# Sparse attention and a gated MLP on one core: the scores of batches 1 to 3 in three parts instead of four, under another listed order

## The chip, the cores and the metric

The kernel runs on one core of a Trainium2 chip. The metric is the device time of one execution in microseconds (us). Three executions of the kernel before took 216.66, 216.99 and 217.43 us, so the median is 216.99 us.

The engines are named as the profile names them: PE is TensorE (matmuls and transposes), PEld its weight loads, ACT is ScalarE, DVE is VectorE, POOL is GpSimd and SP is SyncE. In this kernel POOL issues the loads from HBM, and SP issues the stores and a set of moves inside the chip. Each engine has its own instruction queue and executes it in order; between engines only semaphores order the work.

## The reference

```python
B, H, S, D = q.shape                      # 4, 8, 768, 64
block, window = (32, 16)
k_sum = k.reshape(B, H, nb, block, D).max(axis=3)       # nb = 24
v_sum = v.reshape(B, H, nb, block, D).mean(axis=3)
scores_l = scale * np.matmul(q, k.transpose(0, 1, 3, 2))
mask_l = np.abs(pos[:, None] - pos[None, :]) < window
scores_s = scale * np.einsum('bhsd,bhnd->bhsn', q, k_sum) + np.log(block)
a = softmax(concatenate([where(mask_l, scores_l, -1e9), scores_s]))
attn = np.matmul(a, concatenate([v, v_sum]))
x = attn.transpose(0, 2, 1, 3).reshape(B * S, H * D)    # 3072 x 512
h = x @ w_in                                            # 512 -> 2048
g = h * np.clip(h + 3.0, 0.0, 6.0) / 6.0
out = g @ w_out                                         # 2048 -> 512
```

(The softmax is abbreviated here.) Each query sees the 31 keys around it and 24 block maxima, so the scores are a band and a narrow dense part.

## The kernel before, in words

**Attention.** The 768 queries of a head are cut into `NQ = 12` blocks of `QB = 64`. For a block, `kaug[p]` holds 120 key columns: 96 keys around it (`WIN`) and the 24 block maxima. `p` counts the four pairs of heads. The scores of a block come out with the keys on the partitions; `exp` (ACT) writes them as bf16 into the probabilities `at[p]`, and a multiplication by a band mask (DVE, "masking") zeroes what lies outside the window. `values` multiplies them with `vaug` (values, block sums and a column of ones), divides by the sum on DVE ("recip", "scale") and brings the result into `x`, the transposed input of the MLP. `half` 0 covers blocks 6 to 11, `half` 1 blocks 0 to 5.

Batch 0 has functions of its own (`k_step`, `q_step`, `scores`, `values_first`, `vsum_first`). Batches 1 to 3 use `turn` (tags `w`: 32x32 transposes of keys and queries on DVE, and the maxima), `scores4` (tags `s`, two pairs at once), `vsum` (tags `u4` to `u6`) and `values` (tags `v`).

**MLP.** The 3072 rows are 8 stages `s` of 384 (two per batch). `f1` (tags `F{s}x{ft}`, 16 per stage) is four matmuls into a PSUM bank `h` (there are three), a ReLU on ACT into `r` and the gate on DVE into `g`. `f2` (tags `G{s}{ts}x0`, three per stage, each in four quarters of four matmuls) accumulates in the one bank `o`; a copy and a store by SP follow. For stages 4 to 7 `x` is not made by PE transposes but by a DVE block transpose ("blocks", L642) and 16 small DMAs ("move", L648): four tokens of four DMAs, all on SP's queue. `F4` waits for the moves of batch 2, half 0; `F5`, `F6` and `F7` for the next ones.

**PSUM.** Two double banks `S` serve scores, values, sums and transposes. `scores4` takes both at once.

**The order.** Nothing is scheduled by the compiler. `Plan` records every operation under a tag and a number (`s100.1` is the first `exp` of that score block), and `issue` writes them out in the sequence of the string `ORDER`, which fixes each engine's queue. A suffix `:A` or `:D` picks ACT or DVE where both can do it. Tokens that begin with `-`, `~`, `_` or `=` are matmuls on an idle tile (`keep`, L782), which compute nothing. Loads have tokens too: `K`, `Q` and `V` are keys, queries and values of a batch, `Q0w` the queries of batch 0 for its second half, `I` and `O` the two weight matrices. All of these are on POOL's queue, in the order listed.

Of the kernel before, what the change touches and what calls it, by code (L numbers as in the profile page):

```python
# [29 lines left out]
c.0 K00.0 c.7 c.17 c.6 c.8:A K01.0 c.10:D c.5 c.1 _40 -15 k0.0 k0.2:A c.18 ~1 =2 k1.0 K02.0 ~12 =3 k2.0 k3.0 c.15:D c.2 c.3  # L30
s000.0 k0.3:A c.13:D c.4 c.11:A k1.1 Q00.0 q0.0 k1.4 k0.1 c.20 k1.2:A Q01.0 ~2 =5 q1.0 k0.4 k1.3:D c.9:A c.14:A c.19 k2.3:A
q0.1:A s000.1 q0.2:A =1 s010.0 s010.1 k2.2:A k3.2:D k3.3:D k3.1 V00.0 h000.0:D h001.0:D k2.1 k2.4 s000.2 ~2 =5 v00.0 V01.0 u0.0
h010.0:D s020.0 c.16 s010.2 q1.2:A u0.3:D u0.1:D u0.4:D v01.0 v01.1 v01.2 v00.1 q1.1:A V02.0 h020.0:A h021.0:A h011.0:A v00.2
s020.1 v01.3 v00.3 V03.0 u1.0 u1.3:A h030.0:D s030.0 k3.4 ~2 s030.1 u1.4:D v01.4 h031.0:D Q0w0.0 Q0w1.0 v01.5:D Q0w2.0 =1 q3.0
q3.1:D q2.0 u1.1:A u1.2:D s020.2 v02.0 v02.1 v02.2 s021.0 v02.3 s030.2 v03.0 v03.1 q2.1:A v03.2 s011.0 v03.3 v00.4 v00.5:D v02.4
s021.1 s011.1 s021.2 v03.4 v03.5:D s011.2 v02.5:A s031.0 s031.1 s001.0 s031.2 I2.0 F0x3.0 F0x3.1 F0x3.2 F0x3.3 F0x3.4 F0x3.5
I4.0 F0x6.0 F0x6.1 F0x6.2 F0x4.0 F0x4.1 F0x4.2 F0x4.3 v411.0 v411.1 F0x5.0 F0x4.4 F0x4.5 v411.2 s001.1 I8.0 u0.2:A s001.2 F0x8.0
F0x8.1 F0x8.2 F0x5.1 I0.0 F0x5.2 F0x11.0 F0x1.0 F0x11.1 F0x11.2 F0x1.1 F0x1.2 F0x1.3 F0x1.4 F0x1.5 v410.0 v410.1 F0x7.0 F0x7.1
F0x7.2 v410.2 F0x10.0 F0x10.1 I12.0 F0x13.0 F0x13.1 F0x15.0 F0x15.1 F0x13.2 F0x10.2 v411.3 v411.4:D v410.3 v410.4:A F0x15.2
F0x14.0 F0x14.1 F0x14.2 F0x9.0 F0x9.1 F0x9.2 F0x0.0 F0x0.1 F0x2.0 F0x2.1 K13.0 K10.0 c.12:A F0x0.2 K12.0 K11.0 w10.0 Q1w1.0  # L40
F1x14.0 F1x14.1 F1x14.2 F1x4.0 F1x4.1 F1x4.2 F1x2.0 F1x2.1 F1x2.2 w10.1:D F0x2.2 F0x2.3 F0x2.4 F0x12.0 F0x12.1 F0x12.2 F1x8.0
F1x8.1 F1x8.2 F1x1.0 F1x1.1 F1x1.2 F0x0.3 F0x0.4 F0x0.5 F0x2.5 F1x9.0 F1x9.1 F1x9.2 F1x5.0 F1x5.1 F1x5.2 F1x15.0 F1x15.1 w11.0
w11.2 F1x15.2 w11.3:D Q1w4.0 Q1w2.0 Q1w0.0 w10.2 w10.3:D q6.0 q6.1:A q7.0 q7.1:A F1x7.0 F1x7.1 w11.1:A F1x7.2 F1x12.0 F1x12.1
F1x12.2 O0.0 G02x0.0 Q1w5.0 Q1w3.0 q4.0 q4.1:A q5.0 q5.1:A F1x6.0 F1x6.1 F1x6.2 O1.0 G02x0.1 s100.0 s100.1 s100.3 F1x3.0 w12.0
F1x11.0 F1x11.1 w13.0 w13.2 F1x3.1 F1x11.2 w12.2 w12.1:D O2.0 G02x0.2 s101.0 s101.1 O3.0 F1x10.0 G02x0.3 G02x0.4:A w13.3:D
w13.1:A s101.3 F1x0.0 G00x0.0 G00x0.1 w12.3:D s100.2 s101.2 s100.4 V10.0 h100.0:D F1x10.1 h110.0:A F1x10.2 F1x3.2 s110.0 s110.1
s110.2 s101.4 s110.3 G00x0.2 G00x0.3 G00x0.4:A V12.0 u4.0 h130.0:D h120.0:A F1x0.1 u4.1:D u4.2:A u4.4:D u4.3:D u4.5:D G02x0.5
G01x0.0 G01x0.1 G01x0.2 s110.4 F1x0.2 h111.0:A v100.0 v100.1 v100.2 h121.0:A v101.0 v101.1 v101.2 G01x0.3 G01x0.4:A K20.0 K21.0
K22.0 K30.0 K23.0 w21.0 F1x13.0 F1x13.1 F1x13.2 v100.3 v100.4:A w20.0 w21.3 G12x0.0 w21.2:A v101.3 v101.4:A V22.0 H2.0 h101.0:A
# [764 lines left out]
```

## Time and profile before

| | before |
|---|---|
| median of 3 executions | 216.99 us (216.66 to 217.43) |
| span of the profiled execution, first to last instruction | 215.4 us |
| PE busy | 207.6 us (96%) |
| DVE busy | 162.1 us (75%) |
| ACT busy | 136.0 us (63%) |
| POOL busy | 49.7 us (23%) |
| mean granted TensorE clock | 0.998 |
| read from HBM / written | 28.82 MB / 6.29 MB |

For the profiled execution the page gives the span alone; the span begins with its first instruction and ends with its last, and the median of the timed executions is 1.6 us above it. A busy share is an average over stages. A PE that is "busy" counts the latency of matmuls that overlap, so the pace of PE is better read from the chain of work that ended last: there a group of matmuls has the time by which it held up the next one.

### The profile page before, as it was taken

Reading aid. Unit: us, or ns where it says so; the run is one execution under the profiler, and the core shown is the slowest. Engines: PE = TensorE matmul, PEld = TensorE weight load, DVE = VectorE, ACT = ScalarE, POOL = GpSimd, SP = SyncE. Lnnn points to the kernel's source line nnn. Section 1 sums busy time; section 2 is a strip of 40 time slices with the busy share of each in tenths; the row PEclk is TensorE's granted clock in tenths of the full one; section 3 lists DMA queues with packets and bytes.
Section 4 is the critical chain, followed back from the end, with each engine's and each line's share of the span. In section 5 each row is a group of like instructions: output and inputs, shape, how many; then the busy total and the mean of one; then the engine's idle time right before and its main releaser. Section 6 shows DMA issues by size and latency. Waiting matters only on the chain.

```text
span 215.4 us, 6065 instructions
## 1 busy us (share of the span) xinstructions
PE 207.6 (96%) x2521; PEld 119.9 (56%) x2548; DVE 162.1 (75%) x318; ACT 136.0 (63%) x264; POOL 49.7 (23%) x66
## 2 busy tenths in 40 slices
PE   7999999999999999999999999999999999999993
PEld 7556656655555565565555555555555555564442
DVE  6889889999899999898899889887865555640021
ACT  3879778887898988756578696566345355520110
POOL 7968347905753244000000000000000000000000
PEclk9999999999999999999999999999999999999999
DMA  5999999999999999930334234113314300013123
GB/s 75 161 155 188 204 187 171 191 201 163 204 160 194 181 121 151 107 146 11 37 37 143 27 37 110 49 22 38 70 21 80 76 0 17 34 49 122 52 85 134
DMA packets 91724, 22.68 MB, mean 105 GB/s; under 512 B 82224, under 2 KB 88752, under 8 KB 91696
## 3 DMA queue, kind: packets, MB, share of 16 engines
q0 software_dynamic: 62288, 14.41, 71.9%
q1 hardware_dynamic: 29264, 7.80, 15.3%
q8 instruction: 20, 0.33, 0.6%
q10 hardware_dynamic: 144, 0.07, 0.1%
q14 instruction: 8, 0.07, 0.1%
HBM read 28.82 MB, written 6.29 MB: 163 GB/s over the span
## 4 chain that ended last, share of the span: by engine, by line
PE 82%; SPq 5%; DMA 4%; issue 2%; DVE 2%; POOL 2%; ACT 1%; ACTq 0%; POOLq 0%
PE h L666 36%; PE o L683 29%; PE h L683 5%; SPq L648 4%; DMA first<-in_q_dram 3%; PE S L623 3%; PE S L512 2%; DMA out_dram<-ot 1%; ACT vaug L241 1%; POOL first L305 1%; PE S L636 1%; PE S L666 1%; PE h L581 1%; PE S L489 1%; PE S L553 1%
## 5 line engine op out<-in xcount | busy, mean ns | idle before, releaser
L666 PE MATMUL h<-x,win 128*128 128x384 bf16 x500 | 91.1, 326 | 0.1
L670 ACT ACTIVATE r<-h 128x384 f32<-128x384 f32 x125 | 58.7, 492 | 38.8 <-PE h L666 36.8
L671 DVE SCALAR_TENSOR_TENSOR g<-r,h 128x384 bf16<-128x384 f32 x125 | 65.9, 546 | 22.6 <-ACT r L670 20.0
L683 PE MATMUL o<-wout,g 128*128 128x512 bf16 x309 | 78.0, 379 | 1.9 <-issue 0.8
L666 PEld LDWEIGHTS <-win 128*128 128x128 bf16 x512 | 48.7, 98 | 35.5
L683 PEld LDWEIGHTS <-g 128*128 128x128 bf16 x400 | 38.4, 98 | 37.6 <-issue 0.3
L520 ACT ACTIVATE at<-S 120x768 bf16<-120x768 f32 x24 | 18.6, 810 | 5.5 <-PE S L512 5.4
L241 ACT COPY ot<-o 128x512 f32<-128x512 f32 x17 | 10.0, 587 | 15.4 <-PE o L683 14.2
L521 DVE TENSOR_TENSOR at<-at,mask 96x768 bf16<-96x768 bf16 x24 | 12.6, 549 | 2.0 <-ACT at L520 1.6
L605 DVE TENSOR_TENSOR xn<-S,rc 128x768 bf16<-128x768 f32 x14 | 13.3, 950 | 0.3
L343 POOL DMA_DIRECT2D vaug<-in_v_dram x10 | 11.9, 1194 | 0.4 <-DMA first<-in_k_dram 0.2
L241 DVE COPY ot<-h 128x512 f32<-128x512 f32 x2 | 1.3, 686 | 13.7 <-PE h L683 13.7
L683 PE MATMUL h<-wout,g 128*128 128x256 bf16 (+1 forms) x64 | 11.4, 326 | 0.0
L467 DVE TENSOR_REDUCE red<-kaug 128x24 bf16<-128x768 bf16 x12 | 11.2, 943 | 0.1
L241 ACT COPY vaug<-vaug 32x640 bf16<-32x640 bf16 (+3 forms) x17 | 8.9, 574 | 0.6 <-DMA vaug<-in_v_dram 0.3
L241 ACT COPY vaug<-vs 24x1536 bf16<-24x1536 bf16 x6 | 8.8, 1468 | 0.6 <-DVE vs L241 0.5
L782 PE MATMUL o<-idle 128*128 128x64 bf16 (+2 forms) x70 | 7.5, 287 | 1.1 <-DVE idle L287 1.1
L455 DVE STREAM_TRANSPOSE kaug<-kraw 128x768 bf16<-128x768 bf16 x8 | 8.1, 1025 | 0.3 <-PE S L512 0.3
L623 PEld LDWEIGHTS <-at 120*64 120x64 bf16 x336 | 6.3, 111 | 3.0 <-issue 1.6
L333 POOL DMA_DIRECT2D kraw<-in_k_dram x8 | 5.9, 740 | 8.5 <-DVE kaug L455 7.4
L642 DVE STREAM_TRANSPOSE y<-xn 128x768 bf16<-128x768 bf16 x8 | 7.6, 965 | 0.2
L512 PEld LDWEIGHTS <-kaug 32*128 32x128 bf16 x576 | 5.3, 92 | 4.4 <-issue 3.6
(108 smaller groups left out, 184.2 us busy)
## 6 DMA issues: line engine op xcount, KB each, us to landing
out_dram<-ot SPq DMA_DIRECT2D x19, 256.0 KB, 2.3
vaug<-in_v_dram POOLq DMA_DIRECT2D x6, 384.0 KB, 12.9
wout<-in_moe_w_out_dram POOLq DMA_DIRECT2D x4, 512.0 KB, 9.9
win<-in_moe_w_in_dram POOLq DMA_DIRECT2D x3, 512.0 KB, 10.0
kraw<-in_k_dram POOLq DMA_DIRECT2D x8, 192.0 KB, 12.4
x<-y SPq DMA_DIRECT2D x64, 24.0 KB, 2.0
first<-in_k_dram POOLq DMA_DIRECT2D x6, 192.0 KB, 12.3
first<-in_q_dram POOLq DMA_DIRECT2D x6, 192.0 KB, 12.3
```

What stands on the lines that cost most here:

```text
L241: {"ACT": nc.scalar.copy, "DVE": nc.vector.tensor_copy, "POOL": nc.gpsimd.tensor_copy}[eng](o, i)
L343: op("POOL", "dma128", lambda: nc.gpsimd.dma_start(out=o[BLK:WIN, a:z, 0:D], in_=rows[:, a:z]), w=[("v", b % 2, c) for c in range(lo, hi)] ...
L467: op("DVE", "max", lambda: nc.vector.tensor_reduce(red.slot[:], w[:, :, BLK:WIN].rearrange("p t (n c) -> p t n c", n=2), axis=AX.X, op=ALU ...
L512: nc.tensor.matmul(X[g // 2].slot[:, g % 2, i * QB:(i + 1) * QB], kaug[2 * u + m][rows, t], qT[rows, 2 * u + m, t * QB:(t + 1) * QB], star ...
L520: op("ACT", "exp", lambda a=a, e=e: nc.scalar.activation(a, X[e].slot[0:KEYS, :, 0:HALF], AF.Exp, scale=scl), r=[X[e]], w=[("at", p, half)])
L521: op("DVE", "masking", lambda m=m: nc.vector.tensor_tensor(m, m, mask[:, low(half):low(half) + HQ].unsqueeze(1).to_broadcast([WIN, 2, HQ, ...
L605: nc.vector.tensor_tensor(o, src[..., 0:D], r.unsqueeze(len(r.shape)).to_broadcast(list(o.shape)), op=ALU.mult)
L623: nc.tensor.matmul(X.slot[64 * c:64 * c + 64, i, m:m + D + 1], a[:, t * QB:(t + 1) * QB], vaug[b % 2][0:KEYS, h, t, 0:D + 1], start=True, ...
L666: nc.tensor.matmul(bank(h)[:, 0:HALF], w_in_sb[:, kt, cols], xt[s].slot[:, kt], start=(kt == 0), stop=(kt == NP - 1))
L670: op("ACT", "relu", lambda: nc.scalar.activation(r.slot[:], bank(h)[:, 0:HALF], AF.Relu, bias=0.5, scale=1.0 / 6.0), r=[h], w=[r])
L671: op("DVE", "gate", lambda: nc.vector.scalar_tensor_tensor(gt[s].slot[:, ft], r.slot[:], 1.0, bank(h)[:, 0:HALF], op0=ALU.min, op1=ALU.mul ...
L683: nc.tensor.matmul(o.slot[:, a:z], gt[s].slot[:, ft, ts * 128:(ts + 1) * 128], w_out_sb[:, ft, a:z], start=(ft == 0), stop=(ft == NFT - 1))
```

## The change

`scores4` no longer goes by half and by two pairs. It goes by three parts. Part 0 takes pairs 0 and 1 over blocks 4 to 11, part 1 takes pairs 2 and 3 over the same blocks, and part 2 takes all four pairs over blocks 0 to 3. A part has 64 products of two matmuls in place of 48, fills the 512 columns of both halves of both `S` banks where 384 were filled, and is followed by two `exp` of 1,024 columns where there were two of 768. The masking is on 1,024 columns in parts 0 and 1 (two instructions), and on 512 in part 2 (four). The four tiles `at` become slices of one tile, so that one `exp` of part 2 can write two pairs. The dependencies are kept by three regions of `at`: `values` of half 0 waits for region 0 (parts 0 and 1), of half 1 for regions 1 and 2 (all parts). The copy "around" of the first 16 query columns, which only block 0 needs, now holds up part 2 alone.

Per batch this is 3 score steps in place of 4, 6 `exp` in place of 8, and 8 maskings as before. Over the kernel PE has the same products; there are 65 idle matmuls in place of 80. Where an operation may run on ACT or on DVE, some have changed sides. The whole string `ORDER` is another one. The pieces of it that matter here are shown, with what is left out between them.

```diff
+    THIRD = NQ // 3
-    at = [sb([128, 2, S], BF16, f"at{p}") for p in range(NP)]
+    ats = sb([128, NP, 2, S], BF16, "at")
+    at = [ats[:, p] for p in range(NP)]
...
-           r=[("q", p, 0)], w=[("q", p, 1)])
+           r=[("q", p, 0)], w=[("qa", p)])
+
+    def ats_of(p, half):
+        return [("at", p, x) for x in ((1, 2) if half else (0,))]
...
+    def scores4(b, part):
+        X = [Buf("S"), Buf("S")]
+        us, ts = ((0, 1), (0, THIRD)) if part == 2 else ((part,), (THIRD, NQ))
+        n = (ts[1] - ts[0]) * QB
+        cols = slice(ts[0] * QB, ts[1] * QB)
+        def mms():
+            for u in us:
+                for i, t in enumerate(range(*ts)):
+                    lo = us.index(u) * n + i * QB
+                    for m in range(2):
+                        for g in range(4):
+                            rows = slice(BLK * g, BLK * g + BLK)
+                            nc.tensor.matmul(X[g // 2].slot[:, g % 2, lo:lo + QB], kaug[2 * u + m][rows, t],
+                                             qT[rows, 2 * u + m, t * QB:(t + 1) * QB], start=m == 0, stop=m == 1)
...
+        for e in range(2):
+            ps_ = [2 * u + e for u in us]
+            o = ats[0:KEYS, ps_[0]:ps_[-1] + 1:2, :, cols]
+            op("ACT", "exp1024", lambda o=o, e=e: nc.scalar.activation(o, X[e].slot[0:KEYS].rearrange("p j (u c) -> p u j c", c=n), AF.Exp, scale=scl),
+               r=[X[e]], w=[("at", p, x) for p in ps_ for x in xs])
...
-        for half in range(2):
-            for u in range(2):
-                scores4(b, u, half)
+        for part in range(3):
+            scores4(b, part)
```

The order of the loads of batch 0 and of the first weights, before and after (other tokens left out):

```diff
-K00 K01 K02 Q00 Q01 V00 V01 V02 V03 Q0w0 Q0w1 Q0w2 I2 I4 I8 I0 I12 K13 K10 K12 K11 Q1w1 ...
+K01 K00 Q00 K02 Q01 V00 V01 Q0w1 Q0w0 Q0w2 V02 V03 I0 I4 I12 I8 K10 I2 K13 K11 K12 Q1w5 ...
```

Parts of the new `ORDER`: around the first `F0`, around `u4`, and ahead of `F4`, `F5` and `F6`.

```diff
+... q3.0 v00.1 v01.1 s020.2 q3.1:D s031.0 q2.0 v00.2 v00.3 v00.4 u1.0 I0.0 v01.2 v01.3 h011.0:A s030.2 s031.1 I4.0 s021.0 I12.0
+h020.0:D q2.1:D s001.0 I8.0 h030.0:D v03.0 v02.0 u1.1:A v02.1 v00.5:A u1.3:A v03.1 u1.2:D s001.1 s021.1 h031.0:A u1.4:D s031.2
+K10.0 v02.2 v03.2 v02.3 v03.3 F0x0.0 s011.0 v02.4 v03.4 v02.5:D I2.0 s021.2 K13.0 K11.0 K12.0 Q1w5.0 h021.0:A v01.4 Q1w0.0
+v01.5:D v03.5:D ~1 =1 v411.0 s001.2 F0x6.0 ...
+... s11.0 F1x5.1 s11.3 s11.1 V10.0 G00x0.0 Q20.0 G00x0.1 G00x0.2 G00x0.3 s10.4 h130.0:D s10.2 Q23.0 K22.0 F1x6.1 h120.0:D h121.0:A
+K21.0 F1x5.2 s11.4 h100.0:D s11.2 u4.0 G00x0.4:A h110.0:D u4.1:D u4.2:D u4.3:D G01x0.0 G01x0.1 u4.4:A v100.0 u4.5:D v101.0 ...
+... v201.0 v200.0 F3x10.0 F3x7.0 F3x2.0 G20x0.0 F3x7.1 F3x10.1 v201.1 v200.1 G20x0.1 w20.5:A v201.2 v200.2 v201.3 F3x7.2 F3x2.1
+w21.5:A F3x1.0 s22.0 F3x2.2 v200.3 F3x10.2 w30.1 F3x4.0 F3x1.1 s22.4 F3x4.1 v201.6 v201.7 F3x1.2 w31.0 F3x4.2 F3x9.0 G20x0.2 F3x9.1
+G20x0.3 G20x0.4:D G22x0.5 s22.1 F3x14.0 F3x14.1 s22.5 F3x11.0 s22.3 F3x14.2 s22.2 F3x11.1 w33.0 w31.3 w33.2:A G21x0.0 G21x0.1
+G21x0.2 G21x0.3 s22.6 F3x9.2 G21x0.4:A v201.5 F3x12.0 w31.1 F3x12.1 u6.0 v210.0 u6.1:A u6.4:A v211.0 w30.0 F3x11.2 F3x12.2 F3x8.0
+F3x8.1 F3x8.2 F3x15.0 F3x15.1 F3x15.2 w33.3 w32.0 w33.4:D v201.4 v211.1 G10x0.5 G20x0.5 G32x0.0 F3x13.0 F4x2.0 ...
+... v211.3 G32x0.4:A F4x15.0 F4x0.0 v210.2 ... v210.3 F4x14.0 ... v211.7 v211.4 ... v211.6 v211.5 ... F4x12.1 G31x0.4:A F5x10.0 ...
+... v301.2 G32x0.5 F5x4.0 F5x4.1 G42x0.2 v301.3 ... v301.5 G21x0.5 ... v301.4 ... G42x0.5 v301.7 v301.6 ... F5x12.0 F6x0.0 ...
```

More of the change, by code (lines that the diff above doesn't have):

```diff
@@ L29 @@
 ORDER = """
[L30 to L49, printed above, removed]
@@ new lines @@
+v02.0 u1.1:A v02.1 v00.5:A u1.3:A v03.1 u1.2:D s001.1 s021.1 h031.0:A u1.4:D s031.2 K10.0 v02.2 v03.2 v02.3 v03.3 F0x0.0 s011.0
+v02.4 v03.4 v02.5:D I2.0 s021.2 K13.0 K11.0 K12.0 Q1w5.0 h021.0:A v01.4 Q1w0.0 v01.5:D v03.5:D ~1 =1 v411.0 s001.2 F0x6.0
+u0.4:D s011.1 s011.2 h001.0:D F0x5.0 u0.2:A F0x6.1 F0x0.1 F0x0.2 F0x4.0 F0x0.3 v411.1 F0x5.1 F0x6.2 F0x0.4 Q1w2.0 c.14:A F0x4.1
+F0x4.2 F0x4.3 F0x15.0 F0x15.1 F0x4.4 F0x5.2 F0x0.5 v411.2 F0x12.0 F0x14.0 F0x15.2 F0x12.1 v410.0 Q1w4.0 Q1w3.0 F0x4.5 v410.1
@@ L494, in scores @@
         m = at[p][0:WIN, :, lo:lo + HALF].rearrange("p j (t c) -> p j t c", c=QB)
-        op("ACT", "exp", lambda: nc.scalar.activation(a, X.slot[0:KEYS, :, 0:HALF], AF.Exp, scale=scl), r=[X], w=[("at", p, half)])
+        op("ACT", "exp", lambda: nc.scalar.activation(a, X.slot[0:KEYS, :, 0:HALF], AF.Exp, scale=scl), r=[X], w=ats_of(p, half))
         if not masked:
```

125 lines of the change are left out of this document (66 added, 59 removed).

## The prediction

> **What bounds the kernel now.** I read the page first, then the busy times by stretch, the chain of work that ended last, the groups by form, and the queues of SP, DVE and POOL where the change moves something.
>
> ```profile
> span 215.4 us, 6065 instructions
> PE 207.6 (96%) x2521; PEld 119.9 (56%) x2548; DVE 162.1 (75%) x318; ACT 136.0 (63%) x264; POOL 49.7 (23%) x66
> DVE  6889889999899999898899889887865555640021
> PEclk9999999999999999999999999999999999999999
> ```
> ```profile
> 0.00:12.50 12.50, 10.97 (x157) 7.51 (x157) 9.58 (x32) 8.03 (x16) 10.79 (x21) 1.00 1.12 123
> 12.50:24.40 11.90, 11.30 (x294) 8.13 (x294) 9.86 (x30) 10.06 (x19) 8.06 (x11) 1.00 1.81 182
> 24.40:94.40 70.00, 68.66 (x976) 40.06 (x984) 64.98 (x118) 59.27 (x116) 30.81 (x35) 1.00 1.76 172
> 94.40:117.80 23.40, 23.08 (x337) 12.87 (x342) 21.30 (x40) 14.99 (x27) 0.00 (x0) 1.00 0.29 61
> 117.80:212.20 94.40, 93.60 (x773) 51.30 (x782) 56.07 (x101) 43.37 (x90) 0.00 (x0) 1.00 0.24 54
> ```
> ```profile
> 24.46 2.06 PE h L666 x12
> ...
> 57.77 0.84 PE S L553 x48
> ...
> 68.48 0.48 PE S L512 x48
> ...
> 74.04 0.65 PE h L666 x4
> 74.69 0.86 PE o L683 x4
> ...
> 94.37 0.88 PE S L623 x48
> ...
> 117.83 1.95 PE h L666 x12
> ...
> 210.83 1.32 PE h L683 x12
> ```
>
> The columns of the stretches are: length, busy time of PE, PEld, DVE, ACT and POOL with counts, granted clock, DMA share, GB/s. From 24.4 us on PE is busy 98% or more of each stretch, at a clock of 1.00, and DVE is close behind it up to 117.8 us (64.98 of 70.00, 21.30 of 23.40). The chain gives PE's pace: a group of F 0.65, a quarter of G 0.86, a score block of 48 products 0.48, sums 0.84, two values 0.88. With these I sum all PE work listed from the first F to the end: 128 F 83.2, G 83.0, 12 score blocks 5.8, 14 values 6.2, sums, transposes and the last batch-0 scores 6.3, together 184.5 us. The chain has 212.15 - 24.46 = 187.7 us for it. So 3.2 us are gaps, and the rest of the span is the start (24.46) and the tail. The change adds and removes no PE product, so it can gain in the start and in those gaps alone, and it loses wherever PE has to wait anew.
>
> **The change, part by part.**
>
> *Scores in three parts.* PE: 12 blocks of 48 become 9 of 64, 9 x 0.64 = 12 x 0.48, no change in products. ACT and DVE:
>
> ```profile
> L520 ACT ACTIVATE at<-S 120x768 bf16<-120x768 f32 x24 | 18.6, 810 | 5.5 <-PE S L512 5.4
> L521 DVE TENSOR_TENSOR at<-at,mask 96x768 bf16<-96x768 bf16 x24 | 12.6, 549 | 2.0 <-ACT at L520 1.6
> L241 ACT COPY qT<-S 128x768 bf16<-128x768 bf16 x4 | 3.0, 802 | 0.3 <-PE S L439 0.3
> L241 ACT COPY qT<-S 128x384 bf16<-128x384 bf16 x2 | 0.9, 482 | 0.5 <-PE S L420 0.5
> L512 PEld LDWEIGHTS <-kaug 32*128 32x128 bf16 x576 | 5.3, 92 | 4.4 <-issue 3.6 <-DVE g L671 0.4 <-DVE at L521 0.4
> ```
>
> The two copies give 320/384 = 0.83 ns a column, so an `exp` of 1,024 takes 810 + 256 x 0.83 = 1,023 ns (bounds 810 and, by proportion, 1,080). 18 x 1.02 against 24 x 0.81 is 1.0 us less of ACT. ACT has 59.27 of 70.00 us in the densest stretch, so this is idle time: 0 on the path. Masking has as many instructions and columns as before, 12 + 12 for 24, so with any straight line of cost it stays at 13.2 us. What it gains PE is three fewer starts of a score block: the weight loads of L512 sat idle 3.6 us on "issue" over 10 starts, about 0.36 each, of which the chain shows some 0.1 as lost to PE. I take -0.3 (bounds -1.1 and 0). Both `S` banks are now held for two `exp` of 1.02 instead of 0.81, 0.4 us longer, nine times; the new order lists 2.4 us or more of other PE work between a score block and the next user of its banks (1.7 us at the closest place before), so 0 on its own (up to +0.4 at the closest place, if ACT has a ReLU and a copy first; -0.3 where the old order was tight).
>
> *Idle matmuls.* 65 in place of 80, all ahead of the second F group; they fill waits, so 0 either way.
>
> *The loads of batch 0.* Four loads of Q0w (16, 112 and twice 128 KB) go ahead of V02 and V03 on POOL's queue.
>
> ```profile
> L325 POOL DMA_DIRECT2D qwide<-in_q_dram x3: 830/881/890, 10.4 to 12.7; - x3
> ...
> DMA to landing us min/median/max: 7.0/7.6/7.7
> ```
> ```profile
> L343 POOL DMA_DIRECT2D vaug<-in_v_dram x4: 942/948/1027, 6.1 to 8.9; - x4
> ...
> DMA to landing us min/median/max: 7.3/7.8/8.3
> ```
> ```profile
> L495 ACT ACTIVATE at<-S 120x768 bf16<-120x768 f32 x8 | 6.3, 810 | 1.2 <-PE S L489 1.1
> ...
> L241 ACT COPY vaug<-vaug 32x640 bf16<-32x640 bf16 x6 | 4.3, 717 | 0.0
> ...
> L241 ACT COPY vaug<-vaug 32x128 bf16<-32x128 bf16 x6 | 1.7, 290 | 0.0
> ...
> L241 ACT CAST vf<-o 24x128 bf16<-24x128 f32 x2 | 0.5, 258 | 0.1
> ...
> L241 ACT COPY x<-h 128x384 bf16<-128x384 bf16 x1 | 0.5, 472 | 0.0
> ```
>
> Before, the last V landed at 8.9 + 8.3 = 17.2 us and the last Q0w at 12.7 + 7.0 = 19.7. The bytes ahead of the later one are the same in both orders, so now V03 lands at 19.7 and `u1.0` cannot start earlier. From there, in the listed order: `u1.0` 0.80 to 20.5; on ACT a cast 0.26, a copy of x 0.47, a cast 0.26, two `exp` 1.62, `h031` and `h021` 1.01 each, to 25.1, less some 0.2 for overlap; `v411.0` on PE waits for `h021` and takes 0.44; only then `F0x6.0`, at about 25.5. Before, the first F started at 24.46 and `F0x6.0`, its second group, at 25.1. PE work listed ahead of `F0x6.0` is 12.4 us in both, so nothing is made up: +0.4, and with DVE's three copies and a mask in the same place +0.6 (bounds -1.9, if ACT's queue cost nothing beyond V03's own casts and copies, and +0.9). I take +0.6, since each term has a row. The first weights (I0, then I4) land at 21 and 23.6 by the same running sum, ahead of need. So do K1x, Q1w and O: by the landing of the same bytes their margins are 1.5 us and more.
>
> *Around `u4`.* `h130:D` waits for V12 and stands ahead of two score masks, a gate, two halo copies and `u4.1` to `u4.3` on DVE, which `v100` needs. The bytes ahead of V12 are the same as before, so it lands in the same place, about 55 us, and DVE reaches `h130` at about 54. The chain from there to `v100.0` ends about 0.4 us after PE could begin it. I take +0.2 (0 to +0.9).
>
> *The moves of x ahead of F4 to F7.* These are 16 DMAs on SP behind the second "blocks".
>
> ```profile
> 100.03 10.68 SPq L648 DMA_DIRECT2D x<-y  x16
> ...
> 112.28 1.74 SPq L694 DMA_DIRECT2D out_dram<-ot  x3
> 118.78 10.53 SPq L648 DMA_DIRECT2D x<-y  x16
> ```
> ```profile
> L642 DVE STREAM_TRANSPOSE y<-xn x8: 919/978/979, 96.6 to 156.4; 128x768 bf16<-128x768 bf16 x8
> ...
> DMA to landing us min/median/max: 2.0/2.0/3.6
> ```
>
> Before, the last move of stage 4 was issued by 110.7, about 0.67 apiece, and landed by about 112.7, 5 us ahead of F4 at 117.83. In the new order I count PE work from the place of the second "blocks" to the first F. It must cover 0.97 (blocks) + 15 x 0.67 + 2.0 = 13.0 us, and 0.58 for each store listed between the moves. F4: 13.0 of work against 13.6, one store. F5: 13.2 against 13.0. F6: 13.7 against 14.2, two stores. F7: 14.7 against 13.6. DVE may run "blocks" ahead of its place by some tenths, or behind it by as much; so F4 and F6 wait 0 to 1.2 us each and F5 0 to 0.5. While F waits, all G listed behind it waits too, as PE has one queue. I take +0.3, 0 and +0.3, together +0.6 (0 to 2.9).
>
> *The tail.* The last column half is finished by DVE first and ACT second instead of ACT and DVE; either is one copy after the other: 0.
>
> Sum: -0.3 + 0.6 + 0.2 + 0.6 = +1.1 on the span of 215.4, so 216.5. The median of the timed runs is 216.99, 1.6 above that span; on that scale 218.1 us.
>
> **The rivals.**
>
> *Faster: the start shortens.* DVE and ACT have less listed ahead of the first F (by my sum DVE 20 instead of 23 us). If ACT's queue behind V03 takes half of my 4.4 us, `F0x6.0` starts at 23.3 to 24.2, 0.9 or more earlier than before; with the -0.3 that is -1.2 or more, 215.6 us. For it: DVE is as good as full in that stretch (9.86 of 11.90 us), and the banks `S` have more slack later. Against it: V03 is 2.5 us later, and the copies behind it stand in one queue. It decides if `F0x6.0` begins before 24.8 and F4 and F6 do not wait.
>
> *No change.* The moves land just in time and the start's +0.6 is hidden by the gaps of 3.2 us: 216.9 us.
>
> *Much slower: each boundary waits.* If landing takes the 3.6 us of its maximum in place of 2.0, F4, F5 and F6 wait 2.2, 1.4 and 2.1; half of that, with 0.9 at `u4` and 0.6 at the start, less 0.3, is +4; if DVE is ahead by half a microsecond it is +2.6. About 220 us.
>
> *PE's clock.* It is 1.00 in all stretches before, with the idle matmuls in place. If it fell to half while k0 to q1 run (six groups of transposes, about 3 us), those would take 3 us more, half of it behind loads: +1.5 on the forecast, 219.6. The Trainium skill ("TensorE: Matmul & The Clock Gate", Part 1: The HAM clock gate) says that PE's clock drops to half after an idle window of about 3.4 us and comes back after as long a busy one. By that page fewer fillers speak against this change; an estimate from its figure is up to 1.7 us for one window. No row before shows a drop, and I find no pause above 1.5 us between the listed groups: 3 in 100, inside the case before.
>
> **How the numbers follow.** Forecast (+0.7 to +2.1, 217.7 to 219.1): 0.40. Much slower: 0.15. No change: 0.18. Faster: 0.27. A measurement of this kernel cannot tell less than about 0.3%, 0.65 us, from no change: slower 0.40 + 0.15 = 0.55, same 0.18, faster 0.27. The range runs from 215.6, the middle of the faster case, to 220.2, just above the middle of the much slower one, which leaves out about 0.13 and 0.07.
>
> **What will show it.** In the changed profile: L520's successor at 1.0 us x18; the first F group of four at about 25.5 with `u1` at 19.8; PE idle ahead of an F group with SP's moves ending 2 us earlier, at stages 4 and 6; and the gaps of the rest at 3 us as before. I am wrong if F0 starts before 24.8, if SP's moves end 3 us and more ahead of F4, or if a wait appears that I have not named, on `S` behind the longer `exp` above all.

## The result, and the profile after

The changed kernel takes 226.49 us (median of four executions, 224.85 to 226.58), the kernel before 216.82 beside it: a ratio of 1.0418, 95% interval 1.0375 to 1.0462. It is slower by 9.7 us. (Some executions fall into a second, slower state, and ratios here leave these out: two of the four with a store moved, below.) The prediction had slower as its likeliest side, but 218.1 us as the time and 220.2 as the upper end.

The profiled execution of the changed kernel is its quickest, 224.85 us with a span of 223.1, against 215.4 before: 7.7 us more. The other three have spans of 224.7 to 224.9 at a lower mean clock (0.945 to 0.962 against 0.976), so the trace shows about 7.7 of the 9.7 us; the rest comes with a lower clock, in executions of which there is no trace. One slip in the words on the change, on record above: a score step has 64 matmuls (48 before), each with a weight load, not 64 products of two.

The page of the changed kernel, its head, the busy times, the slices of the granted clock, and the queue of instruction fetches:

```profile
span 223.1 us, 6041 instructions
...
PE 207.6 (93%) x2510; PEld 120.9 (54%) x2533; DVE 158.5 (71%) x315; ACT 131.9 (59%) x261; POOL 49.7 (22%) x66
...
PEclk9996769999999999999999999999999999999999
...
q8 instruction: 20, 0.33, 0.6%
```

PE is busy for the same 207.6 us. The row of the clock is new: 6, 7 and 6 in the slices from 16.7 to 33.5 us, where the kernel before has 9 throughout.

**How much went where.** Busy time of PE up to `F0x6` (the second F group, at 25.1 us before and 30.0 after). The columns are window, length, PE busy with the count, clock, DMA share, GB/s; the second row of each is the idle matmuls alone. Before:

```profile
0.00:25.10 25.10, 22.97 (x453) 1.00 1.46 154
...
0.00:25.10 25.10, 9.95 (x80) 1.00 1.46 154
```

After:

```profile
0.00:30.02 30.02, 22.52 (x458) 0.86 1.45 158
...
0.00:30.02 30.02, 6.59 (x65) 0.86 1.45 158
```

Three differences come out of these rows. The matmuls that compute something took 22.97 - 9.95 = 13.02 us before and 22.52 - 6.59 = 15.93 after: +2.9, at a clock of 0.86. (The two sets are not quite the same, 393 matmuls against 373: `v411.0` now stands ahead of `F0x6` and three matmuls of an F group behind it. The run with the old start, below, has the new set at full clock in 13.2 us, so some 2.7 of the 2.9 is the clock.) The idle matmuls took 3.4 us less. The time in which PE did nothing went from 25.10 - 22.97 = 2.13 to 7.50 us: +5.4. Together +4.9 us, which is the whole delay of `F0x6`: 2.9 in matmuls that compute, and 2.0 of waiting beyond what the idle matmuls had filled.

The same view in the stretches in which the clock is granted (its changes lie 3.41 us or multiples of it apart in this trace):

```profile
4.25:7.66 3.41, 2.38 (x43) 1.00 1.15 167
7.66:11.07 3.41, 1.87 (x24) 1.00 1.43 160
11.07:14.49 3.42, 2.66 (x77) 1.00 2.38 156
14.49:17.90 3.41, 1.82 (x41) 1.00 2.40 157
17.90:21.31 3.41, 2.89 (x78) 0.50 1.47 199
21.31:24.73 3.42, 3.42 (x63) 0.50 1.24 205
24.73:28.14 3.41, 2.47 (x82) 1.00 1.38 200
28.14:31.56 3.42, 3.42 (x37) 0.50 1.73 184
```

A stretch in which PE is busy for 1.82 of 3.41 us is followed by half clock; so is one of 2.47. But stretches with 1.87, 2.38 and 2.66 are followed by full clock, so the busy time alone doesn't say when the clock falls. Half clock ends here behind a stretch in which PE is busy throughout (3.42); that isn't a rule either, since with V02 and V03 loaded earlier (below) such a stretch, at 21.20 us, is followed by half clock again. In all, 10.2 us are at half.

PE in order of time (start, length, line, out<-in, count, and in brackets the idle time before it and what ended it):

```profile
9.54 0.53 PE L422 MATMUL o<-ident,first 96*64 96x96 bf16 x16 [1.54 <-DMA first<-in_q_dram]
...
16.50 0.85 PE L548 MATMUL o<-vaug,ind 96*32 96x128 bf16 x24 [1.59 <-DVE vaug L284]
...
22.90 1.47 PE L548 MATMUL h<-vaug,ind 96*32 96x128 bf16 x24
...
59.34 0.39 PE L696 MATMUL o<-wout,g 128*128 128x512 bf16 x1
61.37 1.89 PE L696 MATMUL o<-wout,g 128*128 128x512 bf16 x8 [1.64 <-issue]
...
118.97 0.57 PE L636 MATMUL S<-vaug,at 120*64 120x65 bf16 x24 [0.94 <-ACT vs L243]
```

The first two are waits of the start: `q0` for queries, and `u0` for a set-up operation of DVE (`c.8`, L284). The third is `u1`, the same 24 matmuls as `u0` in 1.47 us in place of 0.85, at half clock. Then there are two pauses later on: 1.64 us inside `G00x0`, for which no semaphore is shown, and 0.94 us ahead of `v211`, for the block sums from ACT. 4.9 + 1.64 + 0.94 = 7.5 of the 7.7 us. Nothing else behind `F0x6` is above 0.3 us.

Why `u0` waits is read from DVE's queue, and why the block sums are late from ACT's:

```profile
14.43 0.96 DVE L404 TENSOR_REDUCE red<-h 128x24 bf16<-128x768 bf16 x1 [1.38 <-ACT kaug L243]
...
15.75 0.70 DVE L284 MEMSET vaug<- 32x768 f32 x1
```
```profile
117.79 0.59 ACT L243 COPY ot<-o 128x512 f32<-128x512 f32 x1 [2.66 <-DMA out_dram<-ot]
```
```profile
107.85 5.36 SPq L661 DMA_DIRECT2D x<-y  x8
113.30 0.55 SPq L707 DMA_DIRECT2D out_dram<-ot  x1
113.90 6.50 SPq L661 DMA_DIRECT2D x<-y  x8
```

The zeroes `c.8` need nothing, but stand behind a maximum that waits 1.38 us for ACT's copy of late keys. ACT waits 2.66 us to write a tile `ot` whose store (113.30 on SP) stands behind eight moves; the sums behind it come late.

What the prediction costed in `scores4` itself is in the groups: `exp` and masking.

```profile
L530 ACT ACTIVATE at<-S 120x1024 bf16<-120x1024 f32 x18 | 18.1, 1022 | 4.4 <-PE S L521 4.1
L534 DVE TENSOR_TENSOR at<-at,mask 96x1024 bf16<-96x1024 bf16 x12 | 8.1, 683 | 0.1
L534 DVE TENSOR_TENSOR at<-at,mask 96x512 bf16<-96x512 bf16 x12 | 4.7, 408 | 0.3 <-ACT at L530 0.3
```

### The profile page after: what moved, and what is told of

It is laid out like the page before. It is cut to its first block, busy times and chain, and to the rows that moved or that the text cites. A ratio compares the mean times of both kernels' runs of the same rounds, so it can differ in the third digit from the quotient of the medians.

```text
span 223.1 us, 6041 instructions
## 1 busy us (share of the span) xinstructions
PE 207.6 (93%) x2510; PEld 120.9 (54%) x2533; DVE 158.5 (71%) x315; ACT 131.9 (59%) x261; POOL 49.7 (22%) x66
## 4 chain that ended last, share of the span: by engine, by line
PE 82%; DVE 5%; DMA 4%; issue 3%; ACT 3%; SPq 2%; POOL 0%; DVEq 0%; ACTq 0%; POOLq 0%
PE h L679 36%; PE o L696 30%; PE h L696 5%; PE S L636 3%; PE S L521 3%; SPq L661 2%; DMA out_dram<-ot 2%; ACT kaug L243 2%; DMA first<-in_k_dram 2%; DVE red L404 2%; PE S L679 1%; PE S L649 1%; PE h L594 1%; PE S L441 1%; PE S L566 1%
## 5 line engine op out<-in xcount | busy, mean ns | idle before, releaser
L684 DVE SCALAR_TENSOR_TENSOR g<-r,h 128x384 bf16<-128x384 f32 x124 | 64.5, 543 | 30.6 <-ACT r L683 29.5
L696 PE MATMUL o<-wout,g 128*128 128x512 bf16 x313 | 77.2, 379 | 3.3 <-issue 2.4
L530 ACT ACTIVATE at<-S 120x1024 bf16<-120x1024 f32 x18 | 18.1, 1022 | 4.4 <-PE S L521 4.1
L534 DVE TENSOR_TENSOR at<-at,mask 96x1024 bf16<-96x1024 bf16 (+1 forms) x24 | 12.8, 546 | 0.4 <-ACT at L530 0.3
L696 PE MATMUL h<-wout,g 128*128 128x512 bf16 (+1 forms) x64 | 10.7, 326 | 0.0
L715 DVE COPY ot<-h 128x128 f32<-128x128 f32 x1 | 0.3, 292 | 12.8 <-PE h L696 12.8
L500 ACT ACTIVATE at<-S 120x768 bf16<-120x768 f32 x8 | 6.4, 815 | 3.5 <-PE S L494 3.5
L636 PE MATMUL S<-vaug,at 120*64 120x65 bf16 x336 | 7.5, 200 | 0.9 <-ACT vs L243 0.9
L243 ACT COPY kaug<-h 128x480 bf16<-128x480 bf16 (+3 forms) x15 | 4.6, 385 | 5.9 <-PE h L393 4.5
L243 ACT COPY vaug<-vs 24x1536 bf16<-24x1536 bf16 x5 | 7.3, 1468 | 0.9 <-DVE vs L243 0.8
L243 ACT COPY kaug<-kaug 128x352 bf16<-128x352 bf16 (+1 forms) x22 | 6.7, 354 | 1.9 <-DVE kaug L457 1.8
## 6 DMA issues: line engine op xcount, KB each, us to landing
vaug<-in_v_dram POOLq DMA_DIRECT2D x6, 384.0 KB, 12.8
```

What stands on the lines that cost most here:

```text
L243: {"ACT": nc.scalar.copy, "DVE": nc.vector.tensor_copy, "POOL": nc.gpsimd.tensor_copy}[eng](o, i)
L530: op("ACT", "exp1024", lambda o=o, e=e: nc.scalar.activation(o, X[e].slot[0:KEYS].rearrange("p j (u c) -> p u j c", c=n), AF.Exp, scale=sc ...
L534: op("DVE", f"masking{n}", lambda m=m: nc.vector.tensor_tensor(m, m, mask[:, ts[0]:ts[1]].unsqueeze(1).to_broadcast([WIN, 2, ts[1] - ts[0] ...
L636: nc.tensor.matmul(X.slot[64 * c:64 * c + 64, i, m:m + D + 1], a[:, t * QB:(t + 1) * QB], vaug[b % 2][0:KEYS, h, t, 0:D + 1], start=True, ...
L684: op("DVE", "gate", lambda: nc.vector.scalar_tensor_tensor(gt[s].slot[:, ft], r.slot[:], 1.0, bank(h)[:, 0:HALF], op0=ALU.min, op1=ALU.mul ...
L696: nc.tensor.matmul(o.slot[:, a:z], gt[s].slot[:, ft, ts * 128:(ts + 1) * 128], w_out_sb[:, ft, a:z], start=(ft == 0), stop=(ft == NFT - 1))
```

## The experiments

The theory after the result: the start loses 4.9 us to waits and, through them, to PE's clock; the two later pauses are accidents of the new sequence. The rivals: the three parts themselves cost the time, or the start's loss is made up later.

**The old start.** The 134 tokens up to `F0x6.0` (idle matmuls not counted) in the old sequence, but for a few at the end of the row, with the old idle matmuls; the rest as changed:

```diff
-c.0 K01.0 K00.0 Q00.0 K02.0 c.1 Q01.0 c.2 _40 -12 k1.0 c.5 c.17 ...
+c.0 c.7 K00.0 c.17 c.6 K01.0 ... _40 -15 k0.0 ... k1.0 K02.0 ~12 =3 k2.0 k3.0 ...
 F0x0.0 s011.0 F0x6.0 ...
```

> Edit: the changed kernel with its start (all work up to the unbroken row of F0 matmuls, with the loads of batch 0 and the idle matmuls) in the sequence of the kernel before; everything later keeps the new sequence. Theory 1 (about two thirds of the loss is in the start: work there waits for late loads and blocked set-up, and PE's clock falls): F0x6 begins at 25 to 26 us in place of 30.0, the granted clock shows no slices below 9 in the start, the median falls by 4.5 to 7 us to 219.5 to 222. What is left over the kernel before, 3 to 5 us, is the stall at 59.7 us and the wait at 118 us. Rival A (the score blocks of 1,024 columns cost the time): F0x6 may move but the median stays within 1.5 us of 226.5. Rival B (the profile of the start misleads, since what is late there is made up later): F0x6 begins earlier by 4 us and the median by under 2 us.

It took 220.47 us, ratio 1.0146 (1.0121 to 1.0172): 6.0 us less. Its clock and the two window rows up to `F0x6` at 26.09 us:

```profile
PEclk9999999999999999999999999999999999999999
```
```profile
0.00:26.09 26.09, 23.16 (x473) 1.00 1.45 156
...
0.00:26.09 26.09, 9.95 (x80) 1.00 1.45 156
```

Work 13.2 us, idle 2.9: both as before, within 0.8. The start comes 3.9 us earlier, and that is kept to the end. The pause in `G00x0` is gone too, though nothing was changed there (15 idle matmuls more stand ahead of it), and the wait for the block sums stays (0.76 us at 113.7). Both rivals fall: the start is the larger part, and it isn't made up. Of the 6.0 us, the start is 3.9 by the trace and the pause 1.6.

**More idle matmuls in the changed kernel.** Seven of 512 columns ahead of `q0`, three ahead of `k2`, seven ahead of `u0`, two ahead of `s020.1` and two ahead of `s021.1`. That is 21, two more than the expectation counts:

```diff
-... q0.0 ... k2.0 ... u0.0 ... s020.1 ... s021.1 ...
+... ~7 q0.0 ... ~3 k2.0 ... ~7 u0.0 ... ~2 s020.1 ... ~2 s021.1 ...
```

> Edit: the changed kernel with 19 more idle matmuls of 512 columns (0.215 us each at the full clock) where PE waits in the start: 7 ahead of q0, 3 ahead of k2, 7 ahead of u0 and 2 ahead of s021; nothing else. Theory 1 (the clock falls because PE has idle stretches of up to 1.6 us in the start, and the half clock of 10.2 us costs about 3 us of the 4.9): the granted clock shows at most one stretch at half rate, F0x6 begins at 26.5 to 28 us in place of 30.0, and the median falls by 2 to 5 us to 221.5 to 224.5. Rival A (the waits themselves cost the time, and the clock only slows work that would wait anyway): the clock is full and F0x6 begins at 29.5 us or later, median within 0.8 us of 226.5. Rival B (the fall of the clock has another cause than idle PE): the slices at 6 and 7 stay.

222.28 us, ratio 1.0245 (1.0216 to 1.0273). The median fell by 4.2 us, but not as expected. The trace is of the slowest of its four executions (223.3 us). PE up to `F0x6`, at 30.71 us:

```profile
0.00:30.71 30.71, 25.57 (x479) 0.94 1.48 162
...
0.00:30.71 30.71, 12.36 (x86) 0.94 1.48 162
```

The work is back at 13.2 us, so the clock's 2.7 us were saved, but the idle matmuls grew by 5.8 us and the waits shrank by 2.4 only: they were put on the path. In this trace the gain comes later: the pause in `G00x0` is gone here too, and so is the wait for the sums. So this run doesn't tell what the clock is worth.

**Idle matmuls sized to the waits.** `~5` ahead of `q0`, `~1` ahead of `k2`, `~5` ahead of `u0`:

```diff
-... q0.0 ... k2.0 ... u0.0 ...
+... ~5 q0.0 ... ~1 k2.0 ... ~5 u0.0 ...
```

> Edit: the changed kernel with 11 more idle matmuls of 512 columns, sized to fill about two thirds of the waits and not more: 5 ahead of q0 (1.08 us in a wait of 1.54), 1 ahead of k2 (0.22 in 0.46) and 5 ahead of u0 (1.08 in 1.59). Theory 1 (up to the second F group 2.9 us of the 4.9 are PE's own matmuls at half clock): PE's work other than idle matmuls ahead of F0x6 falls from 15.9 to 13.2 us and F0x6 begins at 27 to 28.2 us in place of 30.0. Rival A (the sequence of the start waits on loads and on ACT and DVE, so that PE's faster matmuls only wait longer): the work falls to 13.2 us, but F0x6 begins at 29 us or later. Rival B (PE's clock falls all the same, as its cause is not the idle time): the work stays above 15 us. Median by theory 1 221.5 to 223.5, as the pause at 59.7 us moves with the 22 more instructions too; by the rivals 223.5 to 226.

222.03 us, ratio 1.0220 (1.0194 to 1.0246), and executions within 1.2 us of each other. `F0x6` at 28.65:

```profile
0.00:28.65 28.65, 23.19 (x469) 0.95 1.45 159
...
0.00:28.65 28.65, 9.30 (x76) 0.95 1.45 159
```

Work 13.9 (from 15.9), idle matmuls 9.3 (from 6.6), waits 5.5 (from 7.5): 1.4 us earlier. That lies between theory 1 and rival A. One stretch of half clock was left (25.9 to 29.3 us). But this doesn't price the clock: in the run with the store moved (below), whose start is as in the changed kernel, `F0x6` began at 28.48, with two stretches at half in place of three. What all six executions share is the clock, 0.990 to 0.992 in place of 0.945 to 0.976. Of the 4.5 us by which the median fell, 1.6 is the pause in `G00x0`, which is gone in this trace. The start is still 28.65 - 25.10 = 3.5 us later than before; how much of this is the clock and how much the sequence is open.

**Fewer idle matmuls in the kernel before.** This asks the prediction's own sentence, that idle matmuls are worth nothing:

```diff
-... k1.0 K02.0 ~12 =3 k2.0 k3.0 ...
+... k1.0 K02.0 k2.0 k3.0 ...
```

> Edit: the kernel before, with its longest row of idle matmuls (12 of 512 columns and one of 192, 2.85 us at 6.9 us, ahead of k2) taken out; nothing else. The prediction said that idle matmuls are worth 0 either way. Theory 1 (they hold PE's clock, and without them a stretch of PE idle for some 2.4 us makes the clock fall to half once or twice in the start): the granted clock shows slices of 5 to 8 between 5 and 25 us, the first F group begins 1 to 4 us later than at 24.4, and the median rises by 1 to 4 us to 218 to 221. Rival A (the claim of the prediction): clock full, median within 0.65 us of 217.0. Rival B (the clock falls, but only while PE waits for loads anyway): slices below 9, median within 0.65 us of 217.0.

219.40 us, ratio 1.0110 (1.0064 to 1.0156): 2.4 us slower, from the removal of 13 matmuls that compute nothing. The wait that takes their place, the clock by stretches, and the two window rows up to `F0x6` at 26.70 us:

```profile
8.58 0.53 PE L391 MATMUL h<-ident,first 96*64 96x96 bf16 x16 [1.47 <-DMA first<-in_k_dram]
...
12.73 0.85 PE L420 MATMUL h<-ident,first 96*64 96x96 bf16 x16 [1.13 <-DMA first<-in_q_dram]
...
26.04 2.12 PE L666 MATMUL h<-x,win 128*128 128x384 bf16 x12
```
```profile
6.82:10.23 3.41, 1.94 (x62) 1.00 1.33 176
10.23:13.64 3.41, 2.28 (x33) 0.50 2.36 153
13.64:17.06 3.42, 3.42 (x46) 0.50 2.42 154
17.06:20.47 3.41, 3.34 (x99) 1.00 1.63 191
```
```profile
0.00:26.70 26.70, 22.46 (x440) 0.87 1.45 157
...
0.00:26.70 26.70, 8.26 (x67) 0.87 1.45 157
```

`k2` now comes a microsecond earlier (8.58 against 9.66), since nothing stands ahead of it, and yet the first F comes at 26.04 in place of 24.39: PE ran at half clock for 6.8 us. One wait of 1.47 us was enough here (in the changed kernel one of 1.54 us, at 8.0, was not). The matmuls that compute something took 22.46 - 8.26 = 14.20 us, 1.2 more than the 13.02 before, and the waits grew by 0.4 beyond the idle matmuls taken out. Together that is the 1.6 us by which both `F0x6` and the end of this trace are later; no pause of PE behind it is above 0.25 us. Theory 1 holds, and it holds in a kernel with four score parts and the old loads.

**The set-up operation earlier.** `c.8` listed behind `c.3`:

```diff
-... c.3 c.9:A ... k3.1 k3.4 c.8:D Q0w1.0 ...
+... c.3 c.8:D c.9:A ... k3.1 k3.4 Q0w1.0 ...
```

> Edit: the changed kernel with one set-up operation of DVE (c.8, zeroes in vaug, 0.70 us) listed right after c.3, some 8 us earlier, where DVE waits for a load; nothing else. Theory 1 (u0 waits 1.59 us at 16.5 us because c.8 stands on DVE's queue behind two maxima, which wait for late keys): the wait of u0 falls from 1.59 us to under 0.7 us, and with it PE's later clock may be spared one stretch at half rate: median lower by 0.5 to 3.5 us (223 to 226). Rival (u0 would wait for its values just as long, or the next step takes the wait over): the wait stays above 1.2 us or appears at the next score step, F0x6 within 0.5 us of 30.0, median within 0.5 us of 226.5.

224.29 us, ratio 1.0358 (1.0300 to 1.0416). `u0` waits less than 0.25 us and `F0x6` begins at 28.4. But the run below with a store moved, which leaves the start alone, shows no wait of `u0` either: there half clock came earlier and made the work ahead of `u0` longer, and `F0x6` began at 28.5. So the 2.2 us can't be put down to `c.8`; the verdict is open.

**V02 and V03 ahead of Q0w**, the step on which the prediction's start rested:

```diff
-... Q0w1.0 Q0w0.0 ... Q0w2.0 ... V02.0 V03.0 ...
+... V02.0 V03.0 Q0w1.0 Q0w0.0 ... Q0w2.0 ...
```

> Edit: the changed kernel with the loads V02 and V03 listed ahead of the three Q0w loads, as in the kernel before; nothing else. The step of the prediction (V03 lands 2.5 us later and pushes u1 and the first F0): V03 lands at 17.5 to 18.5 us in place of 20.4, and the median falls by 0.4 to 0.9 us. The theory now (V03 is there before PE reaches u1 at 22.9 us, so its place is worth nothing, and the Q0w loads, later by 2 us, hold q3 and q2 up instead): F0x6 within 0.5 us of 30.0 or up to 1.5 us later, median from 0.3 us faster to 1.5 us slower.

225.33 us, ratio 1.0377 (1.0361 to 1.0392): 1.2 us below the changed kernel, with intervals that touch. V03 lands at 17.9 us in place of 20.4, as said, and in the profiled execution `F0x6` still begins later, at 31.1. The median lies outside both expectations (0.9 us less at most by the one, 0.3 by the other); the landing is right in the first, `F0x6` in the second. What is certain is that the place of V03 isn't what costs 4.9 us.

**All later instructions shifted.** 24 idle matmuls of 64 columns ahead of `q0` and 24 ahead of `u0`, 96 PE instructions with their weight loads. (The expectations speak of bursts of 256 instructions; by the counts a score step is 64 matmuls and 64 weight loads, so 128.)

```diff
-... q0.0 ... u0.0 ...
+... _24 q0.0 ... _24 u0.0 ...
```

> Edit: the changed kernel with 48 more idle matmuls of 64 columns, 24 ahead of q0 and 24 ahead of u0, where PE waits; with their weight loads these are 96 more PE instructions, so that every later instruction stands at another place in the blocks of 256 in which PE's instructions are fetched. Theory 1 (the pause of 1.64 us inside G00x0 at 59.7 us, for which no semaphore is shown, is a late instruction fetch behind two bursts of 256): the pause at G00x0 is gone (under 0.3 us), and one of another length may stand at another place. Rival A (G00x0 waits for something of its own, a weight or a tile): the pause stays at 1.4 to 1.8 us at the same instruction. Of the start: 48 x 0.06 = 2.9 us of the 3.1 us of waiting ahead of q0 and u0 is filled, so by the clock theory F0x6 begins at 27 to 29 us in place of 30.0. Median 221.5 to 225 by theory 1, 223.5 to 226.5 by rival A.

223.57 us, ratio 1.0278 (1.0220 to 1.0336). At `G00x0` there is no pause. Another one stands 9 us later:

```profile
67.80 0.68 PE L520 MATMUL S<-qT,kaug 32*128 32x64 bf16 x64
68.42 0.34 PE L678 MATMUL h<-x,win 128*128 128x384 bf16 x1
70.19 1.96 PE L678 MATMUL h<-x,win 128*128 128x384 bf16 x11 [1.44 <-issue]
```

It has the same form: a score step of 64, one matmul, then 1.4 us without a semaphore. In both traces one of the 20 fetches of 16 KB of PE's instructions begins while that score step runs (58.87 us, 0.89 long, and 67.87 us, 0.96 long), and the pause begins within 0.1 us of its end. In the runs that leave the instructions ahead of `G00x0` as they were (`c.8`, V02 and V03, the store) the pause is there, 1.70, 1.62 and 1.95 us. That the pause goes with the place in the instruction stream is shown; that it is the fetch is read from the times, and the other 19 fetches of each trace pass without a pause of that length. In this run PE also waits at `F4` (0.88 us) and `F6` (1.38 us), which the changed kernel doesn't.

**The store ahead of the moves.**

```diff
-... G22x0.4:A H3.1:D ... v201.6 v201.7 ... G20x0.4:D G22x0.5 ...
+... G22x0.4:A G22x0.5 H3.1:D ... v201.6 v201.7 ... G20x0.4:D ...
```

> Edit: the changed kernel with one store (G22x0.5) listed right behind the copy that fills its tile, ahead of the eight moves on SP's queue in place of behind them. Theory 1 (PE's wait of 0.94 us for the block sums at 119.0 us comes from ACT, which was held 2.66 us by that store's late landing): ACT's wait for the store falls below 0.5 us, PE's wait at u6 and the values behind it below 0.3 us, and the median falls by 0.5 to 1.2 us (225.3 to 226). Rival (the values wait just as long for something else, the moves or the last exponentials): PE's wait there stays above 0.6 us and the median within 0.4 us of 226.5.

The wait is gone: ACT copies at once, and PE runs the values of both pairs in one row.

```profile
115.97 1.01 PE L635 MATMUL S<-vaug,at 120*64 120x65 bf16 x48
116.91 1.47 PE L678 MATMUL h<-x,win 128*128 128x384 bf16 x8
```

Its four executions range from 222.05 to 228.21 us, and the ratio, 1.0231 (1.0170 to 1.0292), is too wide to price a wait of 0.94 us. The pause in `G00x0` is there, 1.95 us, as it should be: nothing ahead of it was changed.

**Old start, store and one wait together.** The old start, `G22x0.5` ahead of the moves, and `v411.0` behind `F0x5.0`. Against the run with the old start alone:

```diff
-... I4.0 v411.0 s001.1 ... F0x0.0 s011.0 F0x6.0 ... F0x5.0 u0.2:A ... G22x0.4:A H3.1:D ... G20x0.4:D G22x0.5 ...
+... I4.0 s001.1 ... F0x0.0 s011.0 F0x6.0 ... F0x5.0 v411.0 u0.2:A ... G22x0.4:A G22x0.5 H3.1:D ... G20x0.4:D ...
```

> Edit: the old start in the new sequence (as in the run of 220.47 us) with two more changes: the store G22x0.5 ahead of the moves, and v411.0 behind F0x5.0 in place of ahead of F0x6.0, since it waited 0.73 us there for an exponential. Theory 1 (what is left over the kernel before is such single waits): the waits at 24.6 us (0.73) and at 113.7 us (0.76) go, and the median is 218.6 to 219.6. Rival (other work is late next): at least one of the two waits comes back in another place and the median stays at 219.8 to 220.8.

218.40 us (ten executions), ratio 1.0053 (1.0025 to 1.0081). No slice of the clock is below 9, and no pause of PE behind its first matmul is above 0.52 us. So three edits to the sequence, with the three parts left as they are, take the ratio from 1.0418 to 1.0053. One edit more, `s011.0` behind `F0x6.0`:

```diff
-F0x0.0 s011.0 F0x6.0 ...
+F0x0.0 F0x6.0 s011.0 ...
```

> Edit: the run of 218.40 us (old start, store ahead of the moves, v411.0 behind F0x5.0) with s011.0 behind F0x6.0 in place of ahead of it, since it waited 0.46 us at 24.7 us for a bank that an exponential held. Theory 1 (each such wait of the start is worth its length): the wait there falls below 0.15 us and the median is 217.8 to 218.2, still 0.7 to 1.1 us above the kernel before. Rival (the wait goes to the next step of the start): median within 0.2 us of 218.4.

218.43 us, ratio 1.0048 (1.0022 to 1.0073): the rival. The wait at 24.7 us went, and `q2` waited 0.58 us for its load and F 0.36 us for a gate.

**The three parts in the old sequence.** The last part of a batch where the fourth step was, the turns of pairs 0 and 1 of the next batch behind it:

```diff
-... s101.0 ... s110.0 ... w21.0 ... w20.0 ... s111.0 ...
+... s11.0 ... s12.0 w21.0 ... w20.0 ...
```

> Edit: the scores in three parts, as changed, but written out in the sequence of the kernel before: the three score steps of a batch stand where the first, the third and the fourth of the four stood, the second is gone, and the turns of the pairs 0 and 1 of batches 2 and 3 that stood ahead of the fourth move behind it; load order, idle matmuls and ACT/DVE choices are those of before. Theory 1 (the loss is in the new sequence, its start above all, and the three parts as such cost little): F0x6 at 25 to 25.5 us, full clock, median 215.5 to 218.5. Rival A (the parts of 1,024 columns themselves cost time: both S banks are held for longer, and 256 PE instructions come in a burst): median above 220, with waits at the score steps or the values behind them. Rival B (fewer exponentials free ACT and the kernel gains): below 215.5.

226.84 us, ratio 1.0449 (1.0401 to 1.0496), rival A by its time. DVE ahead of the worse of two waits:

```profile
112.32 1.92 DVE L456 STREAM_TRANSPOSE kaug<-kraw 128x768 bf16<-128x768 bf16 x2 [3.39 <-PE S L520]
114.28 0.95 DVE L468 TENSOR_REDUCE red<-kaug 128x24 bf16<-128x768 bf16 x1
...
118.56 1.41 DVE L533 TENSOR_TENSOR at<-at,mask 96x512 bf16<-96x512 bf16 x4
```
```profile
73.94 1.30 PE L678 MATMUL h<-x,win 128*128 128x384 bf16 x7 [2.47 <-DVE g L683]
...
119.01 1.15 PE L635 MATMUL S<-vaug,at 120*64 120x65 bf16 x24 [3.01 <-DVE at L533]
```

The last part reads keys and queries of all four pairs, so no turn of the next batch can begin before it. DVE sat idle for 3.4 us and then had three turns, two maxima and three gates ahead of the maskings that PE waits for. In the second wait the clock fell too, for 6.8 us. To tell that from a price of the parts themselves, the last parts were listed earlier:

```diff
-... v101.4:A ... s12.0 w21.0 ... w20.0 ... s22.0 (for s211.0) ... s32.0 (for s311.0) ...
+... v101.4:A s12.0 w21.0 ... w20.0 ... s22.0 (for s201.0) w31.0 ... s32.0 (for s301.0) ...
```

> Edit: as the run of three parts in the old sequence, but the last part of a batch is listed earlier (batches 2 and 3: where the second of the four steps stood; batch 1: right behind the values of half 0), so that the turns of the next batch, which must wait for it, stand nearly where they stood before. Theory 1 (what cost 9.7 us in that run is DVE, which sat idle 3.4 us twice for the last part and then ran two turns, the maxima and the maskings in one row ahead of the gates): the two waits of PE, 2.47 us at 73.9 and 3.01 us at 119.0, fall below 0.8 us each, PE's clock keeps full, and the median is 217 to 220. Rival A (the parts of 1,024 columns cost in themselves, wherever they stand): median above 223. Rival B (with the bunching gone the two exponentials and one step fewer per batch pay): below 216.3.

219.45 us, ratio 1.0098 (1.0066 to 1.0130). Theory 1: the bunching, with the clock that fell by it, cost 7.4 of that run's 9.8 us. The four waits that were left were then each given work to cover them:

```diff
-... v100.4:A G12x0.0 v101.3 v101.4:A s12.0 s12.1 w21.0 w21.3 w21.2:A w20.0 ... F2x11.2 w23.0 ... F3x1.2 w22.5:A s22.0 ...
+... v100.4:A v101.3 v101.4:A G12x0.0 s12.0 s12.1 w21.0 w21.3 w21.2:A ... F2x11.2 w20.0 w20.3 w23.0 ... w23.5:A w22.5:A ... s22.0 ...
-... s32.0 s32.4 G42x0.3 G42x0.4:D s32.1 s32.2 s32.3 F5x6.0 F5x6.1 F5x6.2 ...
+... s32.0 s32.4 G42x0.3 G42x0.4:D F5x6.0 F5x6.1 F5x6.2 s32.1 s32.2 s32.3 ...
```

> Edit: the run of 219.45 us (old sequence, last parts early) with four steps moved by a few places: G12x0.0 between v101.4 and s12.0, the turn w20.0 and its maximum behind F2x11.2, the copy w22.5 ahead of v200.2, and the second of the two exponentials of s32 behind the ReLU of F5x6. Theory 1 (what is left, 2.2 us, is waits of PE of 0.3 to 0.8 us around the last parts, each worth its length): the waits of 0.75 us at 65.6, 0.48 at 70.5, 0.33 at 102.0 and 0.40 at 147.7 fall below 0.2 us each, and the median is 217.6 to 218.3. Rival A (with these gone others come in their place): 218.8 to 219.6. Rival B (the three parts pay once nothing waits): below 216.6.

219.61 us, ratio 1.0094 (1.0070 to 1.0118): by its time rival A. Three of the waits went, and PE waited 1.55 us for a gate at 74.2, behind the turn that had been moved.

## Why the prediction was wrong

It forecast +1.1 us on the span, and the profiled execution has +7.7.

- *Scores in three parts, -0.3.* The sizes were right: `exp` took 1,022 ns (1,023 said), the maskings 12.8 us in all. Idle time of the weight loads ahead of a score step fell (2.5 us against 3.6). What the step left out is that the last part holds back all turns of the next batch. In the changed sequence this doesn't show; in the old one it cost over 7 us. With the largest waits taken out, the three parts stand 0.5% (new sequence) and 0.9 to 1.0% (old one) above the kernel before; none was faster. What this rest is isn't shown.
- *Idle matmuls, "they fill waits, so 0 either way".* This is the step that failed. They fill waits, and with that they held the clock: taking 13 of them out of the kernel before cost 2.4 us. In the changed kernel, with 15 fewer and with other waits, the clock fell twice, and PE's matmuls ahead of `F0x6` took 2.9 us more. What the 15 alone are worth there was not measured.
- *The loads of batch 0, +0.6.* V03 lands at 20.4 us (19.7 said), so the load was followed rightly, but it bounds nothing: `u1` begins at 22.9, not 19.7. I followed one late load and took it that nothing else in the start was late. The waits that were there (`q0` for its queries, `u0` for a memset behind a blocked maximum) stand in the new sequence of DVE and PE, which I hadn't walked through. Which of them are worth most was not settled: the memset alone and V03 alone each gave an unclear result; with the whole old start `F0x6` begins 3.9 us earlier.
- *PE's clock, 3 in 100, +1.5.* It fell. The argument against it was that no pause is above 1.5 us. Two were, by little (1.54 and 1.59), but a bound on a single pause was the wrong measure: the second fall came behind a stretch whose longest pause is 0.47 us (at 24.8), and the stretch with the pause of 1.54 us was followed by full clock. The Trainium skill ("TensorE: Matmul & The Clock Gate", Part 1: The HAM clock gate) gives the length of the stretch, and the traces agree (3.41 us); I read its idle window as one in which PE does nothing at all, and the traces show half clock behind stretches with PE busy for 1.82 and 2.47 of 3.41 us.
- *Around `u4`, +0.2.* No wait of PE above 0.3 us stands there. The pause next to it, 1.64 us in `G00x0`, is of a kind that the prediction doesn't have.
- *The moves ahead of F4 to F7, +0.6.* `F4` began at 122.3 without a wait (the row at 121.65 begins with the last group of F3), 1.9 us after the last move was issued, and the boundaries after it show 0.28 us at most. My count of cover was about right, as the runs show in which PE is earlier: 0.33 and 0.88 us at `F4`, 1.38 at `F6`. In the changed kernel PE was late enough for the moves.
- *An unnamed wait.* The store behind the moves was in my rows (SP's queue), but I counted only what it does to the moves, not what the moves do to it: ACT needs its tile back.

The sum on this scale: 2.9 (matmuls, 2.7 of it the clock) + 2.0 (waits beyond idle matmuls) + 1.6 (pause) + 0.9 (store) = 7.5 of 7.7 us. Not one of the four was in the forecast's sum, so the side, slower, came out right for other reasons than the forecast gave.

## What to carry to other kernels

Work that computes nothing can hold the clock for the work that does, as the 13 matmuls worth 2.4 us show: before calling a filler free, put PE's busy time per stretch of 3.4 us beside the granted clock, and time the kernel once without it. A filler longer than its wait stands on the path: in one trace 5.8 us more of idle matmuls shortened the waits by 2.4 only. When a listed order changes, walk each in-order queue through the start and ask of each operation that needs nothing, such as a memset or a store, what blocked one stands ahead of it.
